# State products of two chunks put ahead of the dense products, and one mask step cut in halves

## The chip, the cores and the metric

The kernel runs on one core of a Trainium2 chip. The metric is the device time of one execution in microseconds (us); less is better. In one execution five engines work side by side, each with its own queue of instructions that it takes strictly in order: TensorE (PE, with its weight loads as PEld), VectorE (DVE), ScalarE (ACT), GpSimd (POOL) and SyncE (SP, which issues the transfers). An instruction whose input is not there holds up everything behind it on its engine.

## The reference

Three stages: a decayed linear attention over 2 batches of 8 heads, 768 tokens and 64 channels, then two gated layers over the 1536 tokens that come out.

```python
for b in range(nb):
    intra = np.einsum('bhic,bhjc->bhij', qb, kb) * Dmask[None]
    intra = np.einsum('bhij,bhjd->bhid', intra, vb)
    inter = np.einsum('bhid,bhde->bhie', qb * lam_pow[None], kv_state)
    out[:, :, sl] = intra + inter
    kv_state = lam_block[None, :, None, None] * kv_state + np.einsum('bhsd,bhse->bhde', kb_dec, vb)
...
a = x @ w_a
b = x @ w_b
x = a * b @ w_out
...
h = np.maximum(np.maximum(x @ w1, x @ w2), x @ w3)
return h @ w_out
```

All of it is computed in float32; the large products are made of three products of a high and a low part each.

## The kernel before

**Attention.** The 768 tokens are cut into six chunks (`m` = 0 to 5) of 128 tokens, and each chunk is worked for both batches (`n` = 2m for the first batch, 2m + 1 for the second). For one chunk TensorE does, in this order: the scores (`scores`, tiles `s`, from chunk 3 on lines 503 and 508); the products of the queries with the state carried so far (`earlier`, line 575, which reads `held`, a part of the tile `stt`); the products of the masked scores with the values (`within`, line 588, into the same banks `o`); and the update of the state (`update`, line 601, bank `k`). Between them the other engines work: `masked` multiplies the scores with the decay mask into `am` (DVE, line 521, one instruction for each half of the heads, `i` = 0 and 1; only for `n` = 0, `i` = 1 does ACT copy the bank and POOL multiply it, line 518); `queries` scales the queries (POOL, line 548); `keys` scales the keys (POOL, line 553); `carry` adds the new bank `k` to `held` (DVE, from chunk 2 on four instructions of line 617, one for each head pair `a`); `taken` copies the banks `o` out (ACT).

**Dense products beside it.** The first layer's first columns need only the first three chunks' tokens. `plain_group` (line 753, banks `p`) is a generator that makes twelve full-width products at each step. The loop over the chunks 3, 4 and 5 draws from it with `next(layer1)`: two steps in chunks 3 and 4, one in chunk 5 and one behind it. A step's result is taken by ACT (`z`) or by DVE (`g`, line 760).

**The order of the helpers' work.** Splitting the weights and the inputs into high and low parts, and their sums for the later products (`x0s`, `x0S`, `wd`, `w`, `hi`, `lo`), are tasks. A planner, `Pace`, keeps a time for each engine in its head; every `pace.pe(...)` moves TensorE's time on, and `pump` then writes down as many task steps as it thinks an engine can take. A step that may run on either of two engines goes to the one that would be done first by the planner's numbers. So the place in the program at which `pace.pe` is called decides on which engine a step stands and in which place. `pace.open` opens a gate that a task waits at while it is planned. The loop at the heart of this, in chunks 3 to 5:

```python
for n in pair(m):
    scores(n)
    masked(n)
for _ in range(1 if last else 2):
    next(layer1)
results(m, last)
for n in pair(m):
    earlier(n)
for n in pair(m):
    within(n)
```

Of the kernel before, what the change touches and what calls it, by code (L numbers as in the profile page):

```python
# [15 lines left out]
ALU = mybir.AluOpType  # L16
# [153 lines left out]
def decay_attention_gated_mlps(ctx: ExitStack, tc: tile.TileContext, qkv: bass.AP, lam: bass.AP, wup: bass.AP, wdown: bass.AP, out: bass.AP):  # L170
    nc = tc.nc
# [6 lines left out]
    pace = Pace()  # L178

    def slot(name, dt=F32):  # L180
        return sp.tile([128, 1536], dt, tag="s", name=name)
# [7 lines left out]
    def rd(t):  # L189
        return t.bitcast(F32)  # L190

    def tt(e, o, a, b, op):
        (nc.vector if e == "DVE" else nc.gpsimd).tensor_tensor(out=o, in0=a, in1=b, op=op)  # L193

    def copy(o, a):
        nc.scalar.activation(out=o, in_=a, func=AF.Copy)  # L196
# [44 lines left out]
    def converted(m, width, roomy=False):  # L241

        load_to(m)
        double = raw.pop(m)[:, 0:width]
        yield ("ACT",), width + 60, "S"
        if width > WB:
            near = wp.tile([128, width], F32, tag="s", bufs=1, name=f"ws{m}")
            scaled(double, near)  # L250
            yield ("ACT",), width + 60, "S"
        t = slot(f"wd{m}") if roomy else hp.tile([128, 1792], F32, tag="h", name=f"w{m}")
        w = t[:, 0:width]
        below(double, w)
        if width == WB:
            near = t[:, WB:2 * WB]
            yield ("ACT",), width + 60, "S"
            scaled(double, near)
        if m not in BYDVE:
            yield ("ACT",), width + 330, "S"  # L260
            sign(double, w)
        if m > 1:
            load_to(m + 2)
        yield ("DVE",), width, "S"
        joined(near, w)
        if m in BYDVE:
            yield ("DVE",), width, "S"
            signed(near, w)
        return t
# [36 lines left out]
    def up_pair(m, i):  # L306

        o = wop[m] = {}
        if m > 0:
            yield "gate", ("done", m - 1)  # L310
        yield "gate", ("conv", m)
        plain = i < NPLAIN
        t = yield from converted(m, 1024, plain)
        if not plain:
            yield from block_sums(t)
        yield "gate", ("split", m)
        hi, lo = (slot(f"{x}{m}", F32R) if plain else hp.tile([128, 1792], F32R, tag="h", name=f"{x}{m}") for x in ("hi", "lo"))
        for s in (slice(0, 1024), slice(1024, 1792))[0:1 if plain else 2]:
            n = s.stop - s.start
            yield ("ACT",), n, "S"  # L320
            copy(hi[:, s], t[:, s])
            e = yield EITHER, n, "S"
            tt(e, lo[:, s], t[:, s], rd(hi[:, s]), ALU.subtract)
            for x, place in PLACE.items():
                if s.start <= place.start < s.stop:
                    o["B12" if plain and x == "T2" else x] = (hi[:, place], lo[:, place])
        pace.open(("done", m))
        if plain:
            yield "gate", ("late", m)
            last = slot(f"hl{m}", F32R)  # L330
            t6 = t.rearrange("p (a n) -> p a n", a=6)
            e = yield EITHER, 512, "S"
            tt(e, t6[:, 4:6], t6[:, 0:1].to_broadcast([128, 2, 256]), t6[:, 1:4:2], ALU.subtract)
            e = yield EITHER, 256, "S"
            tt(e, t6[:, 0], t6[:, 3], t6[:, 4], ALU.subtract)
            e = yield EITHER, 256, "S"
            tt(e, t6[:, 1], t6[:, 2], t6[:, 0], ALU.subtract)
            for s, names in ((slice(1024, 1536), ("T1", "T3")), (slice(256, 512), ("T4",)), (slice(0, 256), ("T2",))):
                n = s.stop - s.start
                h, l = (last[:, x:x + 256] for x in (0, 256)) if names[0] == "T4" else (hi[:, s], lo[:, s])  # L340
                yield ("ACT",), n, "S"
                copy(h, t[:, s])
                e = yield EITHER, n, "S"
                tt(e, l, t[:, s], rd(h), ALU.subtract)
                for k, x in enumerate(names):
                    o[x] = h[:, 256 * k:256 * k + 256], l[:, 256 * k:256 * k + 256]
# [111 lines left out]
    am, sc, ob, kv, at = {}, {}, {}, {}, {"st": 0.0}  # L458
    xa, xh, xl = {}, {}, {}

    def rows(i):
        return slice(64 * i, 64 * i + 64)

    def pair(m):
        return 2 * m, 2 * m + 1
# [45 lines left out]
    def masked(n):  # L511

        am[n] = slot(f"am{n}")
        for i in range(2):
            o, d = am[n][:, 512 * i:512 * i + 512], decay[:, 4 * i:4 * i + 4].rearrange("p a i -> p (a i)")
            if n == 0 and i == 1:
                copy(o, sc[n][i])
                nc.gpsimd.tensor_tensor(out=o, in0=o, in1=d, op=ALU.mult)
                at["am", n] = max(at["am", n], beside(512, pace.run("ACT", 512, pace.t["PE"])))
                continue  # L520
            nc.vector.tensor_tensor(out=o, in0=sc[n][i], in1=d, op=ALU.mult)
            at["am", n] = pace.run("DVE", 512, pace.t["PE"])
        sc.pop(n)

    def beside(n, after):
        pace.t["POOL"] = max(pace.t["POOL"], after) + pace.cost("POOL", n)
        return pace.t["POOL"]
# [40 lines left out]
    def earlier(n):  # L568

        q = aq[n][:, 1024:1536]  # L570
        for w in range(2):
            for i in range(2):
                for x in range(2):
                    a = 2 * w + x
                    nc.tensor.matmul(  # L575
                        place(n, 4 * i + a), held[rows(i), n % 2, a], q[rows(i), 128 * a:128 * a + 128],
                        start=ob[n][1] == 0 and w == 0, stop=False, skip_group_check=True)
        pace.pe(0.5, max(at["qs", n], at["st"]))
# [401 lines left out]
    with tc.manual_schedule():  # L980
# [71 lines left out]
        def layer1_steps():  # L1052
            for i, j in ((0, 0), (1, 0), (0, 1)):
                if j == 0:
                    ga[i] = slot(f"g{i}")
                yield from plain_group(i, j)
                if (i, j) == (NPLAIN - 1, 0):
                    pace.open(("x0", "S3"))
                    pace.open(("x1", "sums"))
                if j == 1:  # L1060
                    finished1(0, Group("", i, j, None, None))
                    open_to("split", NPLAIN + 1)
            groups = [Group(f"u{i}_{j}", i, j, xo.get, gated) for i, j in plan]
            for i, _ in enumerate(in_slots(groups, each1, finished1)):
                if 7 * len(groups) - i == 3:
                    next(then)
                elif 7 * len(groups) - i == 5:
                    pace.need(gtasks[0, 0][0])
                yield
# [15 lines left out]
        layer1 = layer1_steps()  # L1085
# [107 lines left out]
        for m in range(3, NC):  # L1193
            last = m == NC - 1
            if m == 4:
                load_to(NPLAIN)
                for i in range(2):
                    for n in pair(5):
                        load(n, i)
                load_to(NPLAIN + 1)  # L1200
                open_to("conv", NPLAIN)
                pace.open(("late", 1))
                open_to("split", NPLAIN)
            for n in pair(m):
                queries(n)
            if not last:
                for n in pair(m):
                    keys(n)
            for n in pair(m):
                scores(n)  # L1210
                masked(n)
            for _ in range(1 if last else 2):
                next(layer1)
            results(m, last)
            for n in pair(m):
                earlier(n)
            for n in pair(m):
                within(n)
            if last:
                for n in pair(m):  # L1220
                    for i in range(2):
                        taken(n, xa, part=i)
                        if n % 2 == i == 0:
                            operands(1)
                        x = f"A{n % 2 + 1}{i + 1}"
                        pace.open(("x1", x))
                        steps(xo[1].tasks[x], 2)
            else:
                for n in pair(m):
                    taken(n, xa)  # L1230
            if m == 3:
                pace.open(("x0", "sums"))
            if not last:
                for n in pair(m):
                    update(n)
                carry(m)
            else:
                next(layer1)
# [175 lines left out]
```

## Time and profile before

| what | before |
|---|---|
| time, median of 3 runs (lowest to highest) | 500.21 us (499.57 to 500.47) |
| time of the profiled execution | 499.4 us |
| its span, first to last instruction | 497.6 us |
| PE busy | 493.3 us (99%) |
| DVE, ACT, POOL busy | 343.5, 295.5, 60.3 us |

The span is the part of the execution that the trace shows; 1.8 us lie around it. A row of the timeline below gives the start, the busy time and the number of instructions that follow each other; the idle time just before them stands in brackets, with what ended it. TensorE's products overlap each other in the records, so a row's busy time is longer than the distance to the next row's start.

### The profile page before, as it was taken

To read this page: it belongs to the slowest core of one execution; us is meant where nothing else is said; L and a number is where in the kernel's file an instruction comes from. 1 tells how busy PE (TensorE), PEld (TensorE's weight loads), DVE (VectorE), ACT (ScalarE), POOL (GpSimd) and SP (SyncE) were. 2 spreads that over 40 slices of the span, in tenths; PEclk is the share of its full clock that TensorE was granted. 3 is DMA by queue.
4 is the path that set the end of the run, shared out by engine and by line. 5 is a ranking of instruction groups with operands and counts; after the bars stand their busy time and mean duration, and the time that the engine had idled before them with its cause. 6 is when DMAs were issued, how large, how long until landed. Compare 5 with 4: busy or idle time off the path is not lost.

```text
span 497.6 us, 8202 instructions
## 1 busy us (share of the span) xinstructions
PE 493.3 (99%) x3351; PEld 465.3 (94%) x3351; DVE 343.5 (69%) x536; ACT 295.5 (59%) x464; POOL 60.3 (12%) x58
## 2 busy tenths in 40 slices
PE   9999999999999999999999999999999999999997
PEld 6999999999999999998888888999999999998897
DVE  6779886667657656577364189667867885787962
ACT  3867675654465654679572566545666455576561
POOL 4885201101111110120000000000000000000000
PEclk9999999999999999999999999999999999999999
DMA  8996002222222101315231022002202211120023
GB/s 301 414 413 231 1 0 86 84 86 86 86 86 85 60 8 61 126 65 189 87 95 76 0 84 86 0 1 85 86 1 84 86 63 65 63 65 0 22 107 126
DMA packets 10597, 46.66 MB, mean 94 GB/s; under 512 B 1216, under 2 KB 1472, under 8 KB 8000
## 3 DMA queue, kind: packets, MB, share of 16 engines
q1 hardware_dynamic: 10512, 46.14, 25.2%
q8 instruction: 26, 0.43, 0.4%
q14 instruction: 11, 0.09, 0.1%
q10 hardware_dynamic: 48, 0.00, 0.0%
HBM read 42.99 MB, written 3.15 MB: 93 GB/s over the span
## 4 chain that ended last, share of the span: by engine, by line
PE 99%; POOL 0%; ACT 0%; DVE 0%; issue 0%; POOLq 0%
PE yp L851 20%; PE zu L731 18%; PE zv L731 15%; PE bu L731 9%; PE bv L731 8%; PE p L753 5%; PE out L905 5%; PE xu L731 4%; PE xv L731 4%; PE zo L954 3%; PE o L588 2%; PE bo L954 1%; PE s L496 1%; PE o L575 1%; PE k L601 1%; PE s L503 1%
## 5 line engine op out<-in xcount | busy, mean ns | idle before, releaser
L193 DVE TENSOR_TENSOR lo<-w,hi 128x1024 fp32r<-128x1024 f32 (+2 forms) x39 | 42.5, 1091 | 11.6 <-ACT hi L196 11.4
L196 ACT ACTIVATE hi<-w 128x1024 fp32r<-128x1024 f32 (+2 forms) x40 | 37.4, 935 | 11.5 <-DVE w L193 4.9
L851 PE MATMUL yp<-gh,dh 128*128 128x512 f32 x108 | 42.0, 389 | 0.0
L851 PE MATMUL yp<-gl,dh 128*128 128x512 f32 x108 | 42.0, 389 | 0.0
L851 PE MATMUL yp<-gh,dl 128*128 128x512 f32 x108 | 42.0, 389 | 0.0
L783 POOL TENSOR_TENSOR g<-z1u,z6u 128x384 f32<-128x384 f32 x21 | 22.6, 1076 | 147.6 <-DVE z6u L765 147.6
L193 DVE TENSOR_TENSOR gl<-g,gh 128x512 fp32r<-128x512 f32 x36 | 25.2, 719 | 20.7 <-ACT gh L196 20.7
L239 DVE SCALAR_TENSOR_TENSOR w<-ws,w 128x1024 int32<-128x1024 int32 (+1 forms) x21 | 30.4, 1445 | 8.9 <-ACT w L228 6.8
L228 ACT ACTIVATE w<-wr 128x1024 f16<-128x1024 f32 (+2 forms) x26 | 33.1, 1273 | 0.2
L193 DVE TENSOR_TENSOR w<-w 128x256 f32<-128x256 f32 (+1 forms) x57 | 30.6, 538 | 1.3
L223 ACT ACTIVATE w<-wr 128x1024 int32<-128x1024 uint16 (+2 forms) x26 | 27.5, 1057 | 2.4 <-DVE lo L193 2.0
L765 DVE TENSOR_TENSOR z6u<-bu,z6u 128x384 f32<-128x384 f32 x21 | 11.7, 555 | 23.7 <-PE bu L731 23.7
L196 ACT ACTIVATE z6u<-zu 128x384 f32<-128x384 f32 x21 | 10.2, 486 | 27.4 <-PE zu L731 27.4
L196 ACT ACTIVATE gh<-g 128x512 fp32r<-128x512 f32 x36 | 21.4, 622 | 7.5 <-PE yp L851 7.5
L231 ACT ACTIVATE ws<-wr 128x1024 f32<-128x1024 f32 (+1 forms) x22 | 24.2, 1098 | 0.8 <-DMA wr<-wup_dram 0.8
L196 ACT ACTIVATE z7u<-zu 128x384 f32<-128x384 f32 x21 | 10.3, 492 | 23.5 <-PE zu L731 23.4
L851 PEld LDWEIGHTS yp<-gh,dh 128*128 128x128 f32 x108 | 20.3, 188 | 4.2
L851 PEld LDWEIGHTS yp<-gl,dh 128*128 128x128 f32 x108 | 20.3, 188 | 4.2
L851 PEld LDWEIGHTS yp<-gh,dl 128*128 128x128 f32 x108 | 20.3, 188 | 4.1
L731 PE MATMUL bu<-x1S,hi 128*128 128x384 f32 x88 | 22.3, 334 | 0.0
L731 PE MATMUL zu<-x1S,hi 128*128 128x384 f32 x88 | 22.3, 334 | 0.0
L731 PE MATMUL zu<-x1A,hi 128*128 128x384 f32 x84 | 21.3, 334 | 0.0
(260 smaller groups left out, 1448.2 us busy)
## 6 DMA issues: line engine op xcount, KB each, us to landing
wr<-wup_dram SPq DMA_DIRECT2D x20, 1024.0 KB, 4.7
wr<-wdown_dram SPq DMA_DIRECT2D x12, 768.0 KB, 4.3
aq<-qkv_dram SPq DMA_DIRECT2D x12, 512.0 KB, 7.8
av<-qkv_dram SPq DMA_DIRECT2D x6, 512.0 KB, 9.0
out_dram<-ob SPq DMA_DIRECT2D x11, 256.0 KB, 2.0
av<-qkv_dram SPq DMA_DIRECT2D x8, 256.0 KB, 8.3
wr<-wup_dram SPq DMA_DIRECT2D x2, 512.0 KB, 8.9
out_dram<-ob SPq DMA_DIRECT2D x2, 128.0 KB, 1.8
```

What stands on the lines that cost most here:

```text
L193: (nc.vector if e == "DVE" else nc.gpsimd).tensor_tensor(out=o, in0=a, in1=b, op=op)
L196: nc.scalar.activation(out=o, in_=a, func=AF.Copy)
L223: nc.scalar.activation(out=w.bitcast(I32), in_=halves[:, :, 1], func=AF.Copy, scale=2.0 ** -13, bias=2.0 ** -14 - 0.5)
L228: nc.scalar.activation(out=o[:, :, 1], in_=high(double), func=AF.Copy, scale=2.0 ** -112)
L231: nc.scalar.activation(out=near, in_=high(double), func=AF.Copy, scale=2.0 ** -112)
L239: nc.vector.scalar_tensor_tensor(out=w, in0=near, scalar=3, in1=w, op0=ALU.logical_shift_left, op1=ALU.bitwise_or)
L731: nc.tensor.matmul(ps, w, x, start=p in FIRST and i == 0, stop=i == len(todo) - 1, skip_group_check=p not in FIRST)
L753: nc.tensor.matmul(ps, w, x, start=m == 0, stop=m == 11)
L783: nc.gpsimd.tensor_tensor(out=ga[g.n][:, tokens(g.j, 0)], in0=g.z[1], in1=g.z[6], op=ALU.mult)
L851: nc.tensor.matmul(ps[e], w[:, cols], g, start=k == 0 and m == 0, stop=k == K1 - 1 and m == 2)
L905: nc.tensor.matmul(ps, a[:, o:o + 128], w[:, s], start=k == 0 and n == 0, stop=k == K2 - 1 and n == 2)
L954: nc.tensor.matmul(ps, x[:, 128 * r:128 * r + 128], w, start=p in FIRST and n == 0, stop=n == 8, skip_group_check=p not in FIRST)
```

## The change

Three edits. In chunks 3 and 4 the calls of `results` and `earlier` come ahead of the two steps of `layer1` and not behind them; in chunk 5 the order stays. The mask step of `n` = 0, `i` = 1 is made in two halves of 256 columns, so that ACT copies and POOL multiplies twice. And a gate keeps the last piece of the second weight pair's sums (`T2`) back until the group that still reads what it overwrites has been written down.

```diff
@@ up_pair
             for s, names in ((slice(1024, 1536), ("T1", "T3")), (slice(256, 512), ("T4",)), (slice(0, 256), ("T2",))):
                 n = s.stop - s.start
+                if names[0] == "T2":
+                    yield "gate", ("plain", m)
@@ masked
             if n == 0 and i == 1:
-                copy(o, sc[n][i])
-                nc.gpsimd.tensor_tensor(out=o, in0=o, in1=d, op=ALU.mult)
-                at["am", n] = max(at["am", n], beside(512, pace.run("ACT", 512, pace.t["PE"])))
+                for s in (slice(0, 256), slice(256, 512)):
+                    copy(o[:, s], sc[n][i][:, s])
+                    nc.gpsimd.tensor_tensor(out=o[:, s], in0=o[:, s], in1=d[:, s], op=ALU.mult)
+                    at["am", n] = max(at["am", n], beside(256, pace.run("ACT", 256, pace.t["PE"])))
                 continue
@@ layer1_steps
                 if (i, j) == (NPLAIN - 1, 0):
+                    pace.open(("plain", i))
@@ the loop over chunks 3 to 5
-            for _ in range(1 if last else 2):
+            if last:
                 next(layer1)
             results(m, last)
             for n in pair(m):
                 earlier(n)
+            if not last:
+                for _ in range(2):
+                    next(layer1)
             for n in pair(m):
                 within(n)
```

On TensorE, in chunk 4, the program of before has the 24 dense products (banks `p`) between the last scores (`s`) and the products with the state (`o` from `aq` and `stt`):

```order
L508 MATMUL s_1_697<-stt 64x2x64
L753 MATMUL p_726<-xh_201,hi_584 128x384
...
L753 MATMUL p_745<-xl_202,hi_584 128x384
L575 MATMUL o_0_764<-aq_426,stt 64x128 x2
...
L575 MATMUL o_1_765<-aq_428,stt 64x128 x2
L588 MATMUL o_0_764<-am_693,av_430 64x128 x2
```

The changed program has there:

```order
L510 MATMUL s_1_701<-stt 64x2x64
L578 MATMUL o_0_728<-aq_428,stt 64x128 x2
...
L578 MATMUL o_1_729<-aq_430,stt 64x128 x2
L756 MATMUL p_754<-xh_203,hi_590 128x384
...
L756 MATMUL p_777<-xl_204,hi_590 128x384
L591 MATMUL o_0_728<-am_697,av_432 64x128 x2
```

The 16 products with the state moved ahead of the dense ones; chunk 3 has the same move. On DVE the stretch from the last mask of chunk 3 to the four instructions of `carry` that make the state for chunk 4 (`stt` from `k`) reads, before:

```order
L521 TENSOR_TENSOR am_550<-s_1_527,tables 128x512
L760 TENSOR_TENSOR g_445<-p_553,z_459 128x384
L239 SCALAR_TENSOR_TENSOR wd_566<-ws_548,wd_566 128x1024
L760 TENSOR_TENSOR g_445<-p_569,z_474 128x384
L193 TENSOR_TENSOR lo_585<-wd_566,hi_584 128x1024
L193 TENSOR_TENSOR x0s_444<-x_207 128x768
L617 SCALAR_TENSOR_TENSOR stt<-stt,tables,k_629 128x2x64 x4
```

and now:

```order
L524 TENSOR_TENSOR am_552<-s_1_529,tables 128x512
L239 SCALAR_TENSOR_TENSOR wd_573<-ws_550,wd_573 128x1024
L763 TENSOR_TENSOR g_447<-p_575,z_461 128x384
L193 TENSOR_TENSOR lo_591<-wd_573,hi_590 128x1024
L763 TENSOR_TENSOR g_447<-p_593,z_476 128x384
L193 TENSOR_TENSOR x0s_446<-x_209 128x768
L193 TENSOR_TENSOR x0s_446<-x0s_446,x_202 128x768
L620 SCALAR_TENSOR_TENSOR stt<-stt,tables,k_631 128x2x64 x4
```

A second `x0s` of 768 columns, which was POOL's, stands ahead of `carry`, and both `g` stand one place later. In the next such stretch, up to the `carry` for chunk 5, DVE has two more instructions of 768 columns that were POOL's (a `lo` and the third `x0s`). On POOL the five instructions behind the keys of chunk 4 (`av_432`, now `av_434`) were

```order
L553 TENSOR_TENSOR av_432<-av_432,tables 128x512
L193 TENSOR_TENSOR x0s_444<-x0s_444,x_200 128x768
L193 TENSOR_TENSOR wd_566<-wd_566 128x512
L548 TENSOR_TENSOR aq_654<-aq_654,tables 128x512
L548 TENSOR_TENSOR aq_656<-aq_656,tables 128x512
L193 TENSOR_TENSOR lo_784<-w_718,hi_783 128x768
```

and are now

```order
L556 TENSOR_TENSOR av_434<-av_434,tables 128x512
L193 TENSOR_TENSOR wd_573<-wd_573 128x512
L193 TENSOR_TENSOR wd_573<-wd_573 128x256 x2
L551 TENSOR_TENSOR aq_658<-aq_658,tables 128x512
L551 TENSOR_TENSOR aq_660<-aq_660,tables 128x512
L193 TENSOR_TENSOR lo_591<-wd_573,hi_590 128x512
```

The sums of the second weight tile (`wd`) moved to POOL, and to an earlier place.

## Rows read from the trace of the kernel before

**Rows 1.** The page: span, and the chain that ended last, by engine.

```profile
span 497.6 us, 8202 instructions
...
PE 99%; POOL 0%; ACT 0%; DVE 0%; issue 0%; POOLq 0%
```

**Rows 2.** Timeline of PE, first 30 us: start, busy time, line, tile, count.

```profile
0.84 3.57 PE L1003 MATMUL warm_ps<-const-bfloat16-1.0 128*128 128x512 bf16 x8 [0.84 <-PEq L1407]
...
7.77 2.29 PE L588 MATMUL o<-am,av 128*64 128x128 f32 x32
...
14.52 2.05 PE L588 MATMUL o<-am,av 128*64 128x128 f32 x32
```

**Rows 3.** Timeline of the weight loads (PEld), 6 to 17 us.

```profile
8.30 1.51 PEld L588 LDWEIGHTS o<-am,av 128*64 128x64 f32 x28 [0.34 <-POOL am L518]
```

**Rows 4.** Timeline of POOL, first 30 us.

```profile
6.98 1.28 POOL L518 TENSOR_TENSOR am<-am,tables 128x512 f32<-128x512 f32 x1 [3.09 <-ACT am L196]
```

**Rows 5.** Tile av, 4.1 to 5.4 us: issues of chunk 1's values.

```profile
L481 SPq DMA_DIRECT2D av<-qkv_dram x2: 477/604/730, 4.1 to 4.7; - x2
...
DMA to landing us min/median/max: 9.8/10.2/10.7
```

**Rows 6.** Timeline of PE, 26 to 62 us, chunks 4 and 5.

```profile
39.08 0.22 PE L508 MATMUL s<-stt 64*64 64x128 bf16 x2
39.25 0.44 PE L753 MATMUL p<-xh,hi 128*128 128x384 f32 x1
...
43.35 0.34 PE L753 MATMUL p<-xl,hi 128*128 128x384 f32 x1
43.62 1.10 PE L575 MATMUL o<-aq,stt 64*64 64x128 f32 x32
44.65 1.97 PE L588 MATMUL o<-am,av 128*64 128x128 f32 x32
...
51.38 1.10 PE L575 MATMUL o<-aq,stt 64*64 64x128 f32 x32
```

**Rows 7.** Timeline of DVE, 26 to 62 us.

```profile
32.89 1.31 DVE L239 SCALAR_TENSOR_TENSOR wd<-ws,wd 128x1024 int32<-128x1024 int32 x1 [0.36 <-DMA av<-qkv_dram]
34.12 0.55 DVE L760 TENSOR_TENSOR g<-p,z 128x384 f32<-128x384 f32 x1
35.43 1.78 DVE L193 TENSOR_TENSOR lo<-wd,hi 128x1024 fp32r<-128x1024 f32 x1 [0.76 <-POOL av L553]
37.14 0.94 DVE L193 TENSOR_TENSOR x0s<-x 128x768 f32<-128x768 f32 x1
38.01 1.11 DVE L617 SCALAR_TENSOR_TENSOR stt<-stt,tables,k 128x128 f32<-128x128 f32 x4
39.04 2.47 DVE L521 TENSOR_TENSOR am<-s,tables 128x512 f32<-128x512 f32 x4
41.44 2.26 DVE L239 SCALAR_TENSOR_TENSOR w<-ws,w 128x1024 int32<-128x1024 int32 x1
43.73 2.11 DVE L193 TENSOR_TENSOR w<-w 128x512 f32<-128x512 f32 x2
...
47.42 1.22 DVE L193 TENSOR_TENSOR lo<-w,hi 128x1024 fp32r<-128x1024 f32 x1
...
49.43 1.11 DVE L617 SCALAR_TENSOR_TENSOR stt<-stt,tables,k 128x128 f32<-128x128 f32 x4
```

**Rows 8.** Timeline of POOL, 26 to 62 us.

```profile
33.06 3.07 POOL L553 TENSOR_TENSOR av<-av,tables 128x512 f32<-128x512 f32 x2
...
40.05 1.32 POOL L193 TENSOR_TENSOR wd<-wd 128x512 f32<-128x512 f32 x1
41.31 3.52 POOL L548 TENSOR_TENSOR aq<-aq,tables 128x512 f32<-128x512 f32 x2
```

**Rows 9.** PE by windows: busy, instructions, granted clock, DMA share, GB/s.

```profile
494.00:496.00 2.00, 0.38 (x4) 1.00 0.77 286
496.00:497.60 1.60, 0.00 (x0) 0.90 0.07 24
```

## What the change was forecast to do

> **What bounds the kernel now.** The page comes first: the chain that ended last is TensorE's for 99% of a span of 497.6 us [rows 1]. What matters is whether TensorE ever waits inside its stretches, which a busy share cannot tell, since the records overlap. So the second view is TensorE's timeline, read by distances between starts. In chunk 4 the 24 dense products run from 39.25 to 43.35 us, 23 distances of 0.178 on average, the products with the state start 0.27 behind the last of them and take 1.03, and the masked products follow [rows 6]. There is no hole there. The one hole that I see behind the warm-up is in the masked products of chunk 0, where the weight loads stood idle for 0.34 us until POOL's mask step was done [rows 3]. Hence the rule for the sum: work of the other engines is free as long as it is in time for TensorE, and each microsecond that TensorE waits is a microsecond of the time.
>
> The third view is DVE's timeline, for the state. The four instructions of `carry` that make the state for chunk 4 run from 38.01 to 39.12 (38.01 + 1.11), those for chunk 5 from 49.43 to 50.54 [rows 7]. The products that read them start at 43.62 and 51.38 [rows 6]: 4.5 and 0.8 us of cover. In chunk 4 that cover is the dense products and nothing else, because the scores' last row starts at 39.08 [rows 6], when the state is hardly ready.
>
> **The change part by part.**
>
> *Mask in halves.* The masked products of chunk 0 start at 7.77, and POOL's step ends at 6.98 + 1.28 = 8.26 [rows 2, 4]; the loads go on at 8.30 [rows 3]. With halves the first 256 columns are ready some 0.7 us earlier (half of POOL's 1.28 is 0.64), well before they are wanted, and the second half by about 8.1. So TensorE runs some 0.3 earlier from there. But what is late next? The second half of chunk 1's masked products needs the values of the chunk's second batch. Their transfer is the second of two issues, at 4.7, and the slower landing takes 10.7: about 15.4 [rows 5]. That row of products starts at 14.52 and takes 2.05 with the last record's tail [rows 2], so its second half starts near 15.45: just when the data land. The transfer hangs on no engine of this stretch, and 0.3 of head start ends in a wait of nearly 0.3. I take 0.05 us of gain, between 0 (it lands no earlier) and 0.3 (it was early).
>
> *The order of the products in chunks 3 and 4, what it saves.* The number of instructions is the same. Before there are three changes of shape: scores to dense, dense to state products (0.27 from 43.35 to 43.62 where 0.17 is the pace), state to masked products. Now the state products follow the scores in the same 64 by 64 shape [rows 6], and dense to masked takes the place of the other two. I price one such change at what the 0.27 is over the pace, 0.1 us, so 0.1 for each chunk and 0.2 for both; no gain at all and 0.35 are the bounds (the row has only one of the three). The Trainium skill (TensorEngine Tiling (Array Packing), Key Properties) says that changing the tiling mode drains TensorE; the trace agrees with its 0.27 against 0.17.
>
> *What it costs in chunk 3.* Here `carry` has an idle DVE in front of it and follows the update of the state; the scores take longer than `carry`. I price this at nothing, with some 0.2 us of room.
>
> *What it costs in chunk 4.* Now the state products are wanted right behind the scores: at 39.25 less the 0.15 saved so far, 39.1, and they would be through 1.03 later, at 40.1. The state's last piece is then late by what stands ahead of `carry` on DVE. The stretch runs unchanged up to the `lo` of 1024 columns (35.43 to 37.14, the next start; held by the weights' conversion on ACT, not by TensorE) [rows 7]. Behind it now stand one `g` (0.47: its 0.55 less the overlap of some 0.08 that the next starts show), and two `x0s` of 0.87 each (37.14 to 38.01) instead of one. So without anything else `carry` starts at 37.14 + 0.47 + 0.87 + 0.87 = 39.35 and ends at 40.46. Its third and fourth piece are wanted by the third of eight groups of state products, so some 0.8 of that work still follows the last piece: 41.26, which is 1.2 us late.
>
> And there is something else. POOL now makes the sums of `wd` (512 columns and twice 256) in just these microseconds; the 512 ones took 1.32 [rows 8], when DVE worked on masks from a PSUM bank. The rows say that a DVE step with two SBUF inputs and a POOL step do not run together: the `lo` of 1024 columns took 1.78 beside POOL's `av`, which ended at 36.13 (33.06 + 3.07), and 1.22 with POOL idle; the first 1024-column step behind the masks took 2.26, beside POOL's `aq` [rows 7, 8]. They take turns. So: `lo` until 37.2, POOL's 512 columns until 38.4, first `x0s` until 39.2, POOL's 256 columns (half of 1.32, so 0.66) until 39.9, second `x0s` until 40.75, `carry` until 41.75, state products through at 42.55: 2.45 late. The bounds are 1.2 and 2.45; I take 2.2, since the row of `lo` is a collision of just this kind.
>
> The Trainium skill (SBUF — State Buffer, Who interferes with whom) says the same as a rule: a VectorE step with two SBUF inputs and a GpSimd step that reads SBUF share a port that is locked for a whole instruction. By the rule the sum is 2.45, by plain queueing 1.2; the trace's 1.78 against 1.22 speaks for the rule.
>
> *What it costs in chunk 5.* There the order of the products stays, and the question is whether the 0.8 us of cover last. From the end of one `carry` to the start of the next DVE needed 49.43 - 39.12 = 10.3 [rows 7]. It now has two more steps of 768 columns (1.74), and POOL's collisions go from two (some 1.1 on the 2.26 and 1.0 on the 2.11) to one or two: 11.0 to 12.0. TensorE needs from the end of `carry` to the state products of chunk 5: 0.8 for the rest of chunk 4's, 4.4 for the dense ones, and 51.38 - 44.65 = 6.7 as before, so 11.9 [rows 6]. The first piece is there 0.33 after the start of `carry`: anything from in time to 0.5 late. Behind it stand the masks of chunk 5, 2.47 long [rows 7]; the last of them would then be wanted 2.3 after the state products begin and be there 3.5 after `carry` begins. That can cost up to 1.4 in all; I take 0.45, and 0 as the lower bound.
>
> *The gate* only keeps a 256-column piece back; it is wanted much later, beside a full row of dense products. Nothing.
>
> **Sum.** 2.2 + 0.45 - 0.2 - 0.05 = 2.4 us. The profiled execution took 499.4 us, 1.8 more than its span; it becomes 501.8. The median of the runs shown is 500.21, 0.8 above the profiled one, so I forecast 502.6 us, slower by 0.5%. About 0.2% (1.0 us) is what a measurement of this kernel can tell from no change.
>
> **The rivals.**
>
> *The state is in time.* Then only the gains are left: 0.25, or 0.65 with both bounds, so 499.6 to 500.0. It decides at one point: the first piece of `carry` must be done by about 39.2 and the last by 39.4. In the profile of before it just would be (39.12), which speaks for it; the order of DVE's instructions, with one more `x0s` and a later `g` ahead, speaks against it: at least 1.3 us too late. Chance 0.07, 0.04 of it with over 0.2% of gain.
>
> *Only queueing.* POOL's sums of `wd` fall into the gaps, chunk 5 keeps its cover: 1.2 - 0.25, so 501.2 us, on the edge between no change and slower. For it: POOL is free from 36.13 on and might begin before the `lo`. Against: that would only move the collision onto the `lo`. Chance 0.20, half of it within 0.2%.
>
> *Chunk 5 stalls in full.* Both state products wait, and the masks behind: 2.45 + 1.4 - 0.25 = 3.6, so 503.8 us. For it: DVE has no idle time left between the two `carry`. Chance 0.15.
>
> *The clock.* A wait of some 2 us could make TensorE's clock fall from 2.4 to 1.2 GHz. The granted clock was still 1.00 in the 2 us in which the last products ended, and 0.90 in the window behind [rows 9], with no products in it at all. At the start the eight warm-up products came 0.43 apart [rows 2], 512 columns at the lower level. Were the next five microseconds at that level, 2.5 us more would go: 505 us. TensorE would not be idle for longer than at the end of the run. Chance 0.05.
>
> The forecast itself has the rest, 0.53. Sorted by sign: faster 0.04, within 0.2% 0.13, slower 0.83. The range from 500.9 to 504.0 takes in the queueing rival and the full stall of chunk 5, and leaves out the clock and the state in time.
>
> **What the profile after would show.** If right: on TensorE a hole of 1.5 to 2.5 us between the scores of chunk 4 and its state products, put down to DVE's `stt`; the `carry` for chunk 4 starting past 40; an `x0s` on DVE that takes 1.3 or more beside a POOL step on `wd`; no hole at 8.3 and a new one of 0.2 to 0.3 at 15.4, and the same number of products behind. If there is no hole in chunk 4, the sum is wrong in its largest term; if the hole is there and the time is not longer, then TensorE has slack later that the rows do not show.

## The result, and the profile after

In the comparison the changed kernel took 502.83 us (median of 5 runs, 502.3 to 503.2) and the kernel before 499.77 us (5 runs, 499.57 to 500.47). The ratio is 1.0056, with a 95% interval from 1.0042 to 1.0069: slower by 0.56%, some 2.8 us (the two medians lie 3.06 us apart). The forecast was 502.6 us. The profiled execution took 503.2 us, with a span of 501.5 us against 497.6.

The page of the profile after: the span, and the chain that ended last, by engine.

```profile
span 501.5 us, 8200 instructions
...
PE 91%; DMA 4%; POOL 2%; issue 1%; DVE 1%; SPq 1%; POOLq 0%
```

Before, the chain was TensorE's for 99% [rows 1]. Now it leaves TensorE for other engines, so there are stretches in which TensorE was held up. TensorE's timeline says where.

```profile
16.14 1.97 PE L591 MATMUL o<-am,av 128*64 128x128 f32 x32 [1.70 <-DVE w L239]
...
40.47 0.22 PE L510 MATMUL s<-stt 64*64 64x128 bf16 x2
42.17 1.56 PE L578 MATMUL o<-aq,stt 64*64 64x128 f32 x32 [1.46 <-DVE stt L620]
43.66 0.45 PE L756 MATMUL p<-xh,hi 128*128 128x384 f32 x1
...
48.05 1.97 PE L591 MATMUL o<-am,av 128*64 128x128 f32 x32
...
54.78 1.50 PE L578 MATMUL o<-aq,stt 64*64 64x128 f32 x32
56.20 2.08 PE L591 MATMUL o<-am,av 128*64 128x128 f32 x32
```

There are two holes. The one of 1.46 us in chunk 4 stands between the scores and the state products, and is put down to DVE's `stt`, the state. The state products that follow take 1.49 us to the next start instead of 1.03 [rows 6], since each pair of them waits for its own piece of `carry`. The other hole, 1.70 us at 16.14, is in front of the masked products of chunk 1. The timeline names a DVE instruction there, but the tile `av` says more:

```profile
L483 SPq DMA_DIRECT2D av<-qkv_dram x2: 467/652/837, 4.1 to 4.6; - x2
...
DMA to landing us min/median/max: 11.9/12.0/12.0
```

The values of chunk 1 landed 11.9 to 12.0 us after their issue, at 16.0 and 16.6 us. Before it was 9.8 to 10.7 [rows 5].

DVE's timeline, and below it POOL's, of the stretch that makes the state for chunk 4 (to be read against [rows 7, 8]):

```profile
36.61 1.79 DVE L193 TENSOR_TENSOR lo<-wd,hi 128x1024 fp32r<-128x1024 f32 x1 [0.76 <-POOL av L556]
38.32 0.55 DVE L763 TENSOR_TENSOR g<-p,z 128x384 f32<-128x384 f32 x1
38.79 1.56 DVE L193 TENSOR_TENSOR x0s<-x 128x768 f32<-128x768 f32 x1
40.39 1.38 DVE L193 TENSOR_TENSOR x0s<-x0s,x 128x768 f32<-128x768 f32 x1
41.69 1.11 DVE L620 SCALAR_TENSOR_TENSOR stt<-stt,tables,k 128x128 f32<-128x128 f32 x4
...
53.85 1.12 DVE L620 SCALAR_TENSOR_TENSOR stt<-stt,tables,k 128x128 f32<-128x128 f32 x4
```

```profile
34.23 3.09 POOL L556 TENSOR_TENSOR av<-av,tables 128x512 f32<-128x512 f32 x2
37.28 5.08 POOL L193 TENSOR_TENSOR wd<-wd 128x512 f32<-128x512 f32 x3
```

Behind the `lo` stand the `g` and two `x0s`, and only then the state. Both `x0s` run beside POOL's three sums of `wd` and take 1.56 and 1.38 us, where one alone took 0.94 [rows 7]. `carry` starts 5.08 us after the `lo`; before it was 38.01 - 35.43 = 2.58.

**Where the time went, by stage.** For each kernel of this study I take the starts of TensorE's first instruction of a stage, subtract the start of the same instruction in the trace of before, and then the differences of neighbouring stages. A number is what the stage lost (or won, with a minus) against the trace of before, in us. "To chunk 3" is all up to the first scores of chunk 3 at 27.80; "chunk 3" up to the first scores of chunk 4; "chunk 4" up to its masked products at 44.65; "chunk 5" up to the dense products behind its masked ones at 54.31; "behind" is all the rest.

| kernel | median | to chunk 3 | chunk 3 | chunk 4 | chunk 5 | behind | sum |
|---|---|---|---|---|---|---|---|
| changed kernel | 502.83 | 1.55 | -0.16 | 2.01 | 0.51 | 0.00 | 3.91 |
| the same, once more | 502.3 (1 run) | 0.31 | -0.16 | 2.35 | 0.54 | -0.01 | 3.03 |
| halves alone | 500.45 | 1.11 | 0.00 | 0.00 | 0.12 | 0.00 | 1.23 |
| order alone | 502.65 | 1.49 | -0.16 | 1.84 | 0.57 | 0.00 | 3.74 |
| sums behind the state | 504.55 | -0.06 | -0.16 | -0.16 | 5.10 | 0.18 | 4.90 |
| third sum held back too | 504.57 | 0.66 | -0.16 | -0.16 | 3.68 | 1.57 | 5.59 |
| POOL waits | 504.21 | 0.17 | -0.16 | 1.84 | 3.06 | 0.02 | 4.93 |
| chunk 3 alone | 504.86 | 0.90 | -0.16 | 0.00 | 4.59 | 0.34 | 5.67 |
| chunk 4 alone | 502.26 | 0.30 | 0.00 | -0.16 | 1.86 | 0.96 | 2.96 |
| plan pinned | 501.70 | 0.73 | 0.39 | -0.16 | 0.43 | 1.14 | 2.53 |
| plan pinned, mask whole | 501.95 | 0.23 | -0.16 | 0.33 | 0.88 | 1.15 | 2.43 |
| plan pinned, small sums late | 499.75 | -0.26 | -0.16 | 0.74 | 0.06 | -0.02 | 0.36 |

Every loss is made in the first 75 us; from there to the end the offset stays the same to within 0.02 us. The trace of before is one of its quicker executions (499.4 us, where its runs reach 500.8), so a sum is some tenths more than the difference of the medians.

### The profile page after: what moved, and what is told of

The parts are those of the page before. It is cut to its first block, busy times and chain, and to the rows that moved or that the text cites. A ratio compares the mean times of both kernels' runs of the same rounds, so it can differ in the third digit from the quotient of the medians.

```text
span 501.5 us, 8200 instructions
## 1 busy us (share of the span) xinstructions
PE 493.9 (98%) x3351; PEld 465.5 (93%) x3351; DVE 343.5 (68%) x536; ACT 295.8 (59%) x465; POOL 58.6 (12%) x59
## 4 chain that ended last, share of the span: by engine, by line
PE 91%; DMA 4%; POOL 2%; issue 1%; DVE 1%; SPq 1%; POOLq 0%
PE yp L854 20%; PE zu L734 17%; PE zv L734 15%; PE bu L734 9%; PE bv L734 7%; PE out L908 5%; PE xu L734 4%; PE xv L734 4%; PE p L756 3%; PE zo L957 3%; DMA av<-qkv_dram 2%; DMA aq<-qkv_dram 2%; PE bo L957 1%; POOL aq L551 1%; POOL av L556 1%; PE o L591 1%
## 5 line engine op out<-in xcount | busy, mean ns | idle before, releaser
L193 DVE TENSOR_TENSOR lo<-w,hi 128x1024 fp32r<-128x1024 f32 (+2 forms) x40 | 43.4, 1086 | 11.6 <-ACT hi L196 11.4
L193 DVE TENSOR_TENSOR w<-w 128x256 f32<-128x256 f32 (+1 forms) x57 | 29.1, 510 | 1.3
L768 DVE TENSOR_TENSOR z6u<-bu,z6u 128x384 f32<-128x384 f32 x21 | 11.7, 556 | 23.7 <-PE bu L734 23.7
L196 ACT ACTIVATE z7u<-zu 128x384 f32<-128x384 f32 x21 | 10.3, 491 | 23.0 <-PE zu L734 22.9
```

## The experiments

The theory was that of the forecast: the state comes late on DVE, and TensorE waits for it. The rivals were that the transfer of chunk 1's values, or the order of the products itself, costs the time. Medians in one comparison belong together: before took 500.28 us (17 runs) beside the first four kernels, 499.71 (9) beside the next four, 499.61 (9) beside the two pinned ones, and 499.53 (15) beside the last.

### The two halves of the change, each alone

Halves alone is the kernel before with the mask step of the change; order alone takes it back:

```diff
-                for s in (slice(0, 256), slice(256, 512)):
-                    copy(o[:, s], sc[n][i][:, s])
-                    nc.gpsimd.tensor_tensor(out=o[:, s], in0=o[:, s], in1=d[:, s], op=ALU.mult)
+                copy(o, sc[n][i])
+                nc.gpsimd.tensor_tensor(out=o, in0=o, in1=d, op=ALU.mult)
```

> The kernel before with the mask step in halves alone; the products keep their old order. If the loss comes from the late state in chunk 4 (my theory): the median within 0.3 us of the kernel before, no stall of TensorE at 8.3 us, and what is won there is lost at the masked products of chunk 1. If the halves themselves delay the transfer of chunk 1's values (rival): 1.0 to 1.6 us over before, with that hole at about 16 us as in the changed kernel.

> The changed kernel with the mask step in one piece of 512 columns, as before. If the loss comes from the late state: 2.0 to 3.0 us over the kernel before, with the hole of 1.3 us or more between the scores of chunk 4 and its products with the state. If it comes from the transfer that the halves delay (rival): 0.5 to 1.7 us over before, and the landing of chunk 1's values back at about 15.4 us.

Halves alone took 500.45 us, ratio 1.0008 (0.9997 to 1.0020). Order alone took 502.65 us, ratio 1.0048 (1.0036 to 1.0060), with a hole of 1.29 us in chunk 4, put down to DVE's `stt`. So the loss comes with the new order. Order alone still holds the third edit, the gate, which no run has by itself; the last kernel below has it too and is level with before. The hole in front of chunk 1's masked products is in both traces all the same, with landings of 11.4 to 11.5 and 11.6 to 11.7 us after the issue. It is neither part's mark.

### The same kernel again

> The changed kernel once more, for its trace. If the late landing of chunk 1's values at 16.0 us is chance: here it is earlier or later by some tenths or a whole us, and the hole at about 16 us changes by as much, with the end of the span following. If the change causes it: again at 16.0 within 0.2 us and a hole of 1.6 to 1.8 us. The hole in chunk 4 is the same in both cases, 1.3 to 1.7 us.

```profile
7.94 1.09 PE L591 MATMUL o<-am,av 128*64 128x128 f32 x16 [0.61 <-DMA av<-qkv_dram]
...
14.77 1.97 PE L591 MATMUL o<-am,av 128*64 128x128 f32 x32
...
41.29 1.56 PE L578 MATMUL o<-aq,stt 64*64 64x128 f32 x32 [1.82 <-DVE stt L620]
```

Here the values landed after 10.3 to 10.7 us, and the hole at 16 us is not there; the span is 500.6 us. So that hole comes and goes with the program unchanged. The hole in chunk 4 is 1.82 us, somewhat more than I expected: when TensorE comes to chunk 4 earlier, it waits longer there, because DVE's stretch begins with weights that ACT converts as they land, and not with TensorE: the scores of chunk 4 begin 1.24 us earlier than in the first trace (37.79 and 39.03), and `carry` only 0.88 (40.81 and 41.69). The two losses partly replace each other.

### The sums opened behind the state

```diff
-            if m == 3:
-                pace.open(("x0", "sums"))
             if not last:
...
                 carry(m)
+                if m == 3:
+                    pace.open(("x0", "sums"))
```

> The changed kernel with one line moved: the sums x0s of chunk 4's stretch are opened behind the carry for chunk 4 instead of ahead of it, so that the state is ready before both x0s. If the loss comes from the late state: the hole in chunk 4 is under 0.3 us, and the time is back at the kernel before, within -0.4 to +0.7 us (the upper end if the carry for chunk 5 then comes late). If it comes from the transfer of chunk 1's values (rival): no more than 0.5 us is won against the changed kernel.

TensorE's timeline in chunks 4 and 5, and DVE's:

```profile
38.91 1.06 PE L578 MATMUL o<-aq,stt 64*64 64x128 f32 x32
...
49.36 0.44 PE L756 MATMUL p<-xh,hi 128*128 128x384 f32 x1 [0.58 <-ACT x L196]
...
54.02 2.40 PE L578 MATMUL o<-aq,stt 64*64 64x128 f32 x32 [2.28 <-DVE stt L620]
56.35 2.75 PE L591 MATMUL o<-am,av 128*64 128x128 f32 x32
```

```profile
37.84 1.11 DVE L620 SCALAR_TENSOR_TENSOR stt<-stt,tables,k 128x128 f32<-128x128 f32 x4
38.87 1.78 DVE L193 TENSOR_TENSOR x0s<-x 128x768 f32<-128x768 f32 x1
40.69 1.94 DVE L193 TENSOR_TENSOR x0s<-x0s,x 128x768 f32<-128x768 f32 x1
...
51.05 2.56 DVE L193 TENSOR_TENSOR x0s<-x,x0s 128x768 f32<-128x768 f32 x1
53.54 1.11 DVE L620 SCALAR_TENSOR_TENSOR stt<-stt,tables,k 128x128 f32<-128x128 f32 x4
```

The theory of the hole holds: with `carry` ahead of the sums there is none in chunk 4, and the chunk even wins 0.16 us. But the time is 504.55 us, ratio 1.0088, slower than the changed kernel. My theory did not have that; the rival's "no more than 0.5 us is won" holds for the time, but not for its reason, since the values of chunk 1 landed after 9.6 to 9.7 us here and there is no hole at 16 us. The work did not go away. It stands between the two `carry` now, the third `x0s` takes 2.56 us beside a `lo` on POOL, and the `carry` for chunk 5 starts at 53.54, so that TensorE waits 2.28 us there.

### One sum more held back

```diff
-                if x != "S3" or j == 1:
+                if x not in ("S3", "S4") or j == 1:
...
                 if m == 3:
                     pace.open(("x0", "sums"))
+                else:
+                    pace.open(("x0", "S4"))
```

> The kernel with the sums behind the state of chunk 4, and the third sum of x0 also held back, until the carry for chunk 5 is done. If the 2.3 us hole in chunk 5 came from the x0s of 2.56 us ahead of that carry on DVE: it shrinks to 0.3 to 1.3 us, no hole in chunk 4, and the time falls to 502.3 to 503.8 us. If it came from something else (rival: the products of the update, or ACT): the hole stays over 2 us and the time over 504 us.

The hole in chunk 5 stays at 2.21 us and the time at 504.57, as the rival had it, though not for its reason. The planner filled the free place with two small sums of `wd`, which took as long beside POOL as the `x0s` before them:

```profile
51.55 2.49 DVE L193 TENSOR_TENSOR wd<-wd 128x256 f32<-128x256 f32 x2
53.96 1.12 DVE L620 SCALAR_TENSOR_TENSOR stt<-stt,tables,k 128x128 f32<-128x128 f32 x4
```

### POOL kept off DVE's sums

DVE's order is that of the changed kernel; POOL alone has to wait for the state before it sums `wd`.

```diff
+    mark = const.tile([128, 1], F32, name="mark")
...
+                if m == 4:
+                    nc.gpsimd.tensor_copy(out=mark, in_=held[:, 1, NP - 1, D - 1:D])
```

> The changed kernel with one instruction more: ahead of its sums of wd, POOL copies one element of each row of the last piece of carry, so that it can begin the sums only when the state for chunk 4 is done. DVE's order is the same. If POOL's steps hold up DVE's two x0s (my theory): each x0s takes about 0.95 us instead of 1.56 and 1.38, the hole in chunk 4 shrinks by about 1.0 us, to 0.4 to 0.9, and the time falls to 501.2 to 502.0 us. If the x0s are only queued ahead of carry (rival): the x0s take as long as before, the hole is as in the changed kernel (1.3 to 1.9 us), and the time stays within 0.3 us of the changed kernel.

```profile
38.28 0.94 DVE L193 TENSOR_TENSOR x0s<-x 128x768 f32<-128x768 f32 x1
39.25 0.96 DVE L193 TENSOR_TENSOR x0s<-x0s,x 128x768 f32<-128x768 f32 x1
40.13 1.12 DVE L621 SCALAR_TENSOR_TENSOR stt<-stt,tables,k 128x128 f32<-128x128 f32 x4
...
44.81 3.96 DVE L193 TENSOR_TENSOR w<-w 128x512 f32<-128x512 f32 x3
```

```profile
40.62 1.56 PE L579 MATMUL o<-aq,stt 64*64 64x128 f32 x32 [1.29 <-DVE stt L621]
...
52.38 0.44 PE L757 MATMUL p<-xh,hi 128*128 128x384 f32 x1 [1.37 <-DVE g L764]
...
55.33 1.94 PE L579 MATMUL o<-aq,stt 64*64 64x128 f32 x32 [0.60 <-DVE stt L621]
```

From the first `x0s` to `carry` it is 1.85 us now (40.13 - 38.28) instead of 2.90 (41.69 - 38.79): POOL's sums cost DVE 1.05 us. The Trainium skill (SBUF — State Buffer, Who interferes with whom) says that a VectorE step with two SBUF inputs and a GpSimd step that reads SBUF exclude each other, for a whole instruction; the 0.94 against 1.56 agree.

So the steps on DVE did what the theory said; the hole and the time did not. The hole in chunk 4 fell by less than 1.05, to 1.29 us, since DVE's stretch began later against TensorE: the second `g` started 0.16 us behind the first scores of chunk 4 (37.81 and 37.65), and in the same kernel again 0.35 ahead of them. With this, 2.35 + 0.51 - 1.05 is 1.81, and the chunk lost 1.84. And the time rose to 504.21 us, because POOL's sums met the next sums on DVE: three `w` took 3.96 us, where the changed kernel has 1.61. The `g` that frees the bank of the dense products came 1.37 us late, and the state for chunk 5 after it 0.60.

### One chunk at a time

```diff
-            if last:
-                next(layer1)
+            if m != 3:
+                for _ in range(1 if last else 2):
+                    next(layer1)
...
-            if not last:
+            if m == 3:
```

(and with 4 in place of 3).

> The changed kernel with the products moved in chunk 3 alone; chunk 4 has its old order. If the loss is chunk 4's late state: no hole in chunks 3 and 4, 0.1 us saved, the time within 0.4 us of the kernel before. If the move itself costs wherever it is made (rival): at least 0.6 us over the kernel before, with a hole behind the scores of chunk 3.

> The changed kernel with the products moved in chunk 4 alone; here the second x0s stays on POOL, so that one x0s less stands ahead of carry. If what stands ahead of carry on DVE sets the hole: it is smaller than in the changed kernel by about the one x0s, 0.3 to 1.0 us, and the time is 0.2 to 1.0 us over the kernel before. If the state is late for another reason (rival, such as the update of the state on TensorE or the transfers): the hole stays at 1.3 to 1.9 us and the time at about 502.5 us.

Both went against what I expected. Chunk 3 alone, where the move itself wins 0.16 us and chunk 4 has its old order, is the slowest of all: 504.86 us, ratio 1.0096 (1.0081 to 1.0110). The loss is in chunk 5, whose products nobody had moved:

```profile
49.97 2.60 DVE L193 TENSOR_TENSOR x0S<-x0s,x0S 128x768 fp32r<-128x768 f32 x1
52.50 1.48 DVE L193 TENSOR_TENSOR lo<-w,hi 128x768 fp32r<-128x768 f32 x1
53.90 1.11 DVE L620 SCALAR_TENSOR_TENSOR stt<-stt,tables,k 128x128 f32<-128x128 f32 x4
```

```profile
49.00 2.75 POOL L193 TENSOR_TENSOR x0s<-x,x0s 128x768 f32<-128x768 f32 x1 [6.47 <-DVE x0S L193]
51.72 2.84 POOL L193 TENSOR_TENSOR wd<-wd 128x256 f32<-128x256 f32 x2
```

The move gives the planner another picture of who is free, and it hands POOL and DVE other steps in other places; two that collide stand ahead of the `carry` for chunk 5. Chunk 4 alone has the second `x0s` on POOL, as before. There the state is in time, chunk 4 wins 0.16 us, and 2.8 us go in chunk 5 and behind it: the `lo` and the third `x0s` of 768 columns stand ahead of the `carry` for chunk 5 on DVE, as in the changed kernel, TensorE waits 0.60 us for the state at 52.42 and 0.35 us for `x1A` at 59.36. The time is 502.26 us, ratio 1.0047.

So the order of the products is worth 0.16 us for each chunk, and what costs is the plan of DVE's and POOL's steps that comes with it. The next three kernels test this directly.

### The changed order with the plan of before

The products stay in the changed order, and the steps that the planner had moved are pinned:

```diff
+            if m == NPLAIN and n == 768:
+                yield "gate", ("pin", "S4")
...
-            e = yield EITHER, n, "S"
+            e = yield ("POOL",) if m == NPLAIN and n == 768 else EITHER, n, "S"
...
-            e = yield EITHER, 512, "S"
+            e = yield ("POOL",), 512, "S"
...
+            yield "gate", ("pin", "wd")
...
+                pin = self.name == "x0" and x in ("S2", "S4")
+                if pin:
+                    yield "gate", ("pin", x)
+                e = yield ("POOL",) if pin else EITHER, 768, "S"
...
+            if m > 3:
+                pace.open(("pin", "S2" if m == 4 else "S4"))
...
                 carry(m)
+                if m == 4:
+                    pace.open(("pin", "wd"))
```

> The changed kernel, its products in the changed order, with the other engines' steps held to the plan of before: the second and third sum of x0, the first sum of wd and the lo of 768 columns go to POOL, at the places that they had there, and the small sums of wd stand behind the carry for chunk 5. If the loss lies in what the plan puts on DVE ahead of the two carry (my theory): no hole over 0.4 us behind the scores of chunk 4 nor before the state products of chunk 5, and the time is from 0.4 us under the kernel before to 0.3 us over it. If the order of the products costs by itself (rival): at least 1.5 us over the kernel before, as in the changed kernel.

> The same with the mask step in one piece of 512 columns. If the halves are worth nothing, since what they win at 8.3 us is lost at the landing of chunk 1's values: the median within 0.3 us of the kernel with halves. If they win their head start (rival): 0.3 to 0.5 us slower than that one.

No hole over 0.4 us is left in chunks 4 and 5, as expected, and chunk 4 wins 0.16 us in the first. The time is not: 501.70 us, ratio 1.0043, and 501.95 with the mask in one piece, ratio 1.0048. The halves are again worth nothing that can be told. What is left stands mostly in chunk 5 (0.43) and behind (1.14). One small sum of `wd` took 1.03 us on DVE ahead of the masks of chunk 5, and ACT's copies of its halves stood ahead of `x1A`, on which the last dense products waited (0.37 us at 58.98, in the first of the two):

```profile
55.28 0.62 ACT L196 ACTIVATE hi<-wd 128x512 fp32r<-128x512 f32 x1
56.37 0.42 ACT L196 ACTIVATE hl<-wd 128x256 fp32r<-128x256 f32 x1 [0.46 <-DVE wd L193]
...
57.09 0.85 ACT L196 ACTIVATE x1A<-x 128x768 fp32r<-128x768 f32 x1
```

The last kernel opens this gate later:

```diff
-                if m == 4:
-                    pace.open(("pin", "wd"))
...
                         steps(xo[1].tasks[x], 2)
+                pace.open(("pin", "wd"))
```

> The kernel with the plan held to that of before, and the small sums of wd kept back once more, until the results of the last chunk are taken, so that neither they on DVE nor the copies of their halves on ACT stand ahead of the masks of chunk 5 and of the operands x1A. If the 0.3 and 0.1 us that the plan held to that of before still lost in chunk 5 and the 1.0 behind it came from these (my theory): all of it goes, no hole from 50 to 65 us beyond those of the kernel before, and the time is from 0.4 us under the kernel before to 0.4 us over it. If the loss comes from the products' order (rival): 1.5 us or more over before as there.

It took 499.75 us (11 runs) against 499.53 (15 runs), ratio 1.0004 (0.9995 to 1.0013). The loss is gone with the order of the products as changed. DVE's order just ahead of the two `carry` is that of before, but for the second `g`, which stands behind the `lo` and not ahead of it:

```profile
37.30 0.54 DVE L769 TENSOR_TENSOR g<-p,z 128x384 f32<-128x384 f32 x1
37.77 0.94 DVE L193 TENSOR_TENSOR x0s<-x 128x768 f32<-128x768 f32 x1
38.64 1.11 DVE L623 SCALAR_TENSOR_TENSOR stt<-stt,tables,k 128x128 f32<-128x128 f32 x4
...
50.20 1.12 DVE L623 SCALAR_TENSOR_TENSOR stt<-stt,tables,k 128x128 f32<-128x128 f32 x4
```

```profile
39.12 1.56 PE L581 MATMUL o<-aq,stt 64*64 64x128 f32 x32 [0.21 <-DVE stt L623]
```

With that `g` in front the state is not quite in time: `carry` starts 3.05 us after the `lo` (35.59) where it was 2.58, TensorE waits 0.21 us for it in chunk 4, and the chunk loses 0.74. That eats what the order wins. No version was faster than the kernel before.

## Why the prediction was right, point by point

- **The state in chunk 4** was to cost 2.2 us, less 0.1 for the order. The chunk lost 2.01 us in the profiled execution and 2.35 without the late landing. The split held as far as it was measured: 1.2 was to come from queueing behind the `g` and a second `x0s`, and 1.0 from POOL's sums, for which the runs give 1.05 us; no run gives the queueing by itself. The upper bound, 2.45 by strict turns, was closer than the 2.2 chosen: with the 0.16 that the order wins, the state cost 2.51 us in the changed kernel, once more. The rival of only queueing falls with it. That the state itself is the cause is shown by the sums-behind kernel, in which the hole vanishes while the order of the products stays.
- **The order of the products** was to save 0.1 us a chunk; it saves 0.16, in chunk 3 in nine of the ten traces in which it is moved, and in chunk 4 in the four in which the state is in time.
- **Chunk 3** was to cost nothing, and did so in those nine. In the tenth, the first pinned kernel, the weight loads stood still for 0.36 us in the middle of the state products, which the timeline puts down to issue. The state was ready by then (`carry` ended at 29.77, the products began at 30.03); what held them stays open.
- **Chunk 5** was to cost 0.45 us; it lost 0.51 and 0.54. The `carry` began 11.05 us behind the end of the one before (53.85 - 42.80), where 11.0 to 12.0 were forecast, and the state products took 1.42 us to the next start (56.20 - 54.78) instead of 1.03. The range of 0 to 1.4 was too narrow for what can happen there: other plans of the same steps lost 1.9 to 5.1 us.
- **The mask in halves** was to be worth 0.05 us. Halves alone is level with before. With the changed order the ratio is 1.0056 with halves and 1.0048 without, with the plan pinned 1.0043 and 1.0048: of both signs, and inside the intervals. The head start is there in some traces (0.67 us at the scores of chunk 1 in halves alone), and it is lost at the landing of chunk 1's values. I put that hole at 0.2 to 0.3 us; it was from nothing to 1.8, by chance.
- **The clock** stayed at its upper level in both traces of the changed kernel, whose holes in chunk 4 are 1.46 and 1.82 us. The rival was a real one: other kernels of this study show such a fall, for some 3 us and not five, as the last section tells. One of the changed kernel's five executions (503.09 us) has a mean granted clock of 0.997, as those kernels have; it has no trace, so a fall there is likely but not shown.
- **The sum.** 2.4 us were forecast over before's profile. The changed kernel, once more, lost 3.03 by its trace, without the late landing. Of the 0.6 us between, 0.3 stand ahead of chunk 3, where the transfers of the start differ from one execution to the next, and 0.25 are chunk 4's. That the forecast time, 502.6, came within 0.2 us of the median is in part luck: it stands on a median of 500.21 for the kernel before, which took 499.77 in the comparison, so that 2.4 us of loss were forecast where the medians give 3.06.

What the prediction did not see is why the second `x0s` and the `wd` sums stood there at all. I took the planner's result as given from the order of the instructions, which was enough for the sum, and three remedies failed on it.

## What to carry to other kernels

Where a planner places the steps of two engines by estimated times, moving work on a third engine moves their whole plan. Read the new plan from the start of the move to the next deadlines, and not only at the place of the move: a step taken out of the way of one deadline lands in front of the next when the engines have no idle time between them. And to learn what a move is worth by itself, hold the plan fixed; here it was 0.16 us for a chunk whose state was in time, while the changed plans cost 2 to 5.

## What the runs showed of the hardware

TensorE's granted clock fell behind two of the three longest waits of this study. In chunk 3 alone TensorE waited 2.20 us for the state of chunk 5; windows of its timeline from 54 us (busy time and instructions of PE, PEld, DVE, ACT and POOL, granted clock, DMA share, GB/s):

```profile
54.00:55.00 1.00, 0.62 (x10) 0.63 (x10) 1.00 (x5) 0.41 (x1) 0.56 (x1) 1.00 0.00 0
...
56.00:57.00 1.00, 1.00 (x19) 0.83 (x14) 1.00 (x3) 0.00 (x0) 0.00 (x0) 0.76 0.00 0
57.00:58.00 1.00, 1.00 (x13) 1.00 (x11) 1.00 (x2) 0.38 (x1) 0.00 (x0) 0.50 0.00 0
58.00:59.00 1.00, 1.00 (x13) 1.00 (x12) 1.00 (x3) 0.97 (x2) 0.00 (x0) 0.50 0.00 0
59.00:60.00 1.00, 1.00 (x9) 0.67 (x6) 1.00 (x2) 0.97 (x3) 0.00 (x0) 0.53 0.00 0
60.00:61.00 1.00, 1.00 (x7) 1.00 (x7) 1.00 (x2) 0.97 (x3) 0.00 (x0) 1.00 0.00 0
```

The clock was still at 2.4 GHz when the products went on, and fell to 1.2 GHz some 2 us later, for about 3 us, with the engine busy. In the sums-behind kernel, with a wait of 2.28 us that ended at 54.02, it fell within the first microsecond behind the wait (0.80 from 54 to 55, 0.50 from 55 to 58). The kernel with one sum more held back waited 2.21 us, and its trace has the full clock behind it. From the state products of chunk 5 to the dense ones behind took 5.26 and 5.01 us in the two with the lower clock and 3.88 in the third, a difference of 1.1 to 1.4 us in that stretch. How much of it is left at the end is not shown: behind that stretch the third kernel lost 1.57 us and the other two 0.18 and 0.34, and the medians of the sums-behind kernel and the third are 504.55 and 504.57. In the traces of before, of the changed kernel, both times, of POOL waits and of the last kernel, whose waits are 1.82 us at most, the clock is 1.00 in every window up to 494 us.

The mean granted clock of each execution, most of which have no trace, points to more such falls. It is 0.999 or 1.00 in every execution of the kernel before. It is 0.996 or 0.997 in all five of the sums-behind kernel, in four of five of chunk 3 alone and in two of four of the third. In chunk 3 alone the one execution at 0.999 took 503.32 us, the others 504.58 to 505.50; in the third kernel the two at 0.997 took 505.15 and 504.28 us, the two at 1.00 504.87 and 504.23. Halves alone has 0.997 in one of twelve, its slowest (502.82 us). So part of the time of chunk 3 alone is probably not its waits; for the other two no such part can be told.

The landing of one and the same pair of transfers was 9.2 to 12.0 us behind the issue from one trace to the next, 10.3 and 12.0 with nothing changed in the program.
